# Turned x tiles in PSUM tiles of their own, and the x loads in another place of the queue

## The chip, the cores and the metric

The kernel runs on one core of one Trainium2 chip. The metric is the device time of one execution in microseconds (us), the median of several. A profile is one execution, recorded by the hardware; its "span" is about 1.7 us shorter than the device time of the same execution.

TensorE is called PE in the profile, its weight loads PEld, VectorE DVE, ScalarE ACT, GpSimd POOL, SyncE SP (SPq is its queue, from which most DMAs are issued). The profile also gives the clock granted to TensorE as a share of full speed; "cold" below means half speed.

## The reference, cut to what matters

Two independent computations share the output. A is a diagonal state-space layer, B an attention over segments of 32 tokens with a memory of 8 tokens. Both read an x of 2048 tokens by 1024 features.

```
# A: u = x B^T; h[t] = Lam * h[t-1] + u[t]; y = 2 Re(h C^T) + x * Dskip
# B: per segment: h = concat(mem, x_seg); q, k, v = h Wq, h Wk, h Wv (32 heads of 128)
#    o = softmax(q k^T / sqrt(128) + mask) v;  out = o Wo;  mem = out[:8]
```

Only the first 80 us matter here. There the kernel computes the V projection of B in "V quarters" (512 tokens by 4 heads; `v_x`), each in four PSUM tiles of 128 tokens by 512 columns ("V tiles" 0 to 3), and, interleaved with them, the u of A (`stage1`), whose scan runs on VectorE and whose states go to DRAM (`a_hs`).

## The kernel before

TensorE needs the features of x on the partitions, so x must be turned. For the first 512 tokens of B the kernel loads x plainly (`b_xr`) and turns it on TensorE into PSUM, from where VectorE and ScalarE copy it to `b_xe`. All later quarters of x, for B (`b_xe`) and A (`a_xT`), are turned by DMA transposes issued from SyncE.

```python
# class K: tag "U" has 2 buffers of 4 KiB per partition, "P" has 3 of 2 KiB
def turn_x0(self, i):                      # i = 0..3: 128 tokens each
    k = self.k
    if i % 2 == 0:
        self.xt = k.ps("U", (128, 2, KC, 128), BF16)      # one tile for two turns
    for c in range(KC):
        k.PE.transpose(self.xt[:, i % 2, c, :], self.x0[i][:, c * 128:(c + 1) * 128], k.ident[:])
    for h in range(2):                                     # halves: "v" VectorE, "s" ScalarE
        cs = slice(4 * h, 4 * h + 4)
        k.copy("vs"[h], self.xe[:, cs, 128 * i:128 * i + 128], self.xt[:, i % 2, cs, :])

# v_x, first quarter only:
    ps = [k.ps("P")[:] for _ in range(3)]
    self.turn_x0(0); self.turn_x0(1)
    for i, c in ((0, 0), (0, 1), (1, 0), (1, 1)):
        self.v_mm(ps[i], w, i, 128 * c, 128 * c + 128)     # V tiles 0 and 1, columns 0 to 255
    self.turn_x0(2)
    self.v_mm(ps[0], w, 0, 256, 512); self.v_mm(ps[1], w, 1, 256, 512)
    self.turn_x0(3)
    ps.append(k.ps("U", (128, 2, 512))[:, 0, :])
    self.v_mm(ps[2], w, 2); self.v_mm(ps[3], w, 3)         # V tiles 2 and 3

# check_consts, called late in the program, but hoisted by the scheduler to the start:
    k.fmask = k.cst.tile([L, 2, L], FP32, name="f_mask")
    G.memset(k.fmask[:], 1.0)                              # ... more on GpSimd (G) ...
    V.tensor_scalar(k.fmask[:, 1, :], k.fmask[:, 0, :], 1.0, 1.0e9, ALU.subtract, ALU.mult)   # on VectorE

# the main loop; steps alternate: v v v v, then s v s v ...   ("s" is stage1 of A)
    b.load_x(1)
    # ... consts, parameters ...
    b.v_x(0, 0, wv[0])
    a.load_b(0); a.load_x(0)
    loads = [lambda: b.load_x(2), lambda: a.load_x(1), lambda: a.load_x(2), lambda: b.load_x(3), lambda: a.load_x(3)]
    for kind, pc, q in order[1:]:
        if loads and kind == "v":
            loads.pop(0)()
        # ... v_x, or stage1, which ends with: SP.dma_start(self.hs[tb][:, pc, :, :], h[:])
```

PE and SP are pinned to program order in this phase; the other engines are ordered by the scheduler.

## Time and profile before

| | before |
|---|---|
| device time, median of 3 | 1260.05 us (1259.23 to 1260.36) |
| PE busy | 1239.0 of 1257.7 us |
| PE idle, for copies of turned x | 6.2 us, twice, longest 5.1 |
| PE idle, for the DMA of A's last x quarter | 1.6 us, once |

From the page, the summary of PE:

```profile
PE 1239.0 (99%) x8270; PEld 664.0 (53%) x8342; DVE 668.2 (53%) x1248; ACT 263.7 (21%) x633; POOL 273.4 (22%) x407
```

PE's waits in the kernel before (engine, line, what it would do next, what ended the wait; us in total, times, longest):

```profile
PE psU L62 <- ACT b_xe L87: 6.2, 2, 5.1
PE psU L62 <- DMA a_xT<-in_A_x_dram: 1.6, 1, 1.6
```

The timeline of PE (start us, duration us, what, and in brackets the idle time before it):

```profile
9.03 0.61 PE L62 MATMUL psU<-ident,b_xr 128*128 128x128 bf16 x8
16.47 1.01 PE L62 MATMUL psU<-ident,b_xr 128*128 128x128 bf16 x8 [5.09 <-ACT b_xe L87]
17.70 3.19 PE L62 MATMUL psP<-b_wv,b_xe 128*128 128x512 bf16 x7 [0.22 <-issue]
23.13 0.18 PE L62 MATMUL psR<-ident,a_r 24*128 24x24 bf16 x1
...
77.41 3.63 PE L62 MATMUL psU<-a_xT,a_bt 128*128 128x512 bf16 x16 [1.58 <-DMA a_xT<-in_A_x_dram]
```

After 11.4 us PE idles 5.09 us until a ScalarE copy. The next lines are slow: 8 transposes take 1.01 us that took 0.61 at 9.03; the granted clock is at half from 15.1 to 21.9 us. (At 17.70 one of 8 matmul records is missing, hence "x7"; V tile 2 began near 17.3.) At 77.41 it waits for a_xT.

VectorE, then ScalarE, at the end of that long wait (the same view for each):

```profile
15.29 0.18 DVE L937 TENSOR_SCALAR f_mask<-f_mask 40x40 f32<-40x40 f32 x1 [7.62 <-POOL f_mask L936]
15.38 0.41 DVE L89 COPY b_xe<-psU 128x512 bf16<-128x512 bf16 x1
```

```profile
15.82 0.60 ACT L87 ACTIVATE b_xe<-psU 128x512 bf16<-128x512 bf16 x1 [7.53 <-DVE b_xe L89]
```

Two things are to be seen. ScalarE's half of a copy starts only when VectorE's half has ended (15.38 + 0.41 = 15.79, then 15.82; in the first turn 5.83, then 5.87). The Trainium skill, "PSUM — Partial Sum Buffer" (PSUM bank collisions raise a hardware error), says that two engines must not touch one PSUM bank in the same 32-partition quadrant at once, and that one guards by bank and quadrant (in the simple version by bank), not by address; a turned tile of 8 x 128 bf16 on 128 partitions is one bank of 2 KiB. The trace is in line with such a guard: the halves are never abreast. And the copy at 15.38 is late because VectorE, which works in order, stood 7.62 us in front of `f_mask`, waiting for GpSimd. The skill's "TensorE: Matmul & The Clock Gate" (the engine queue depths in Part 1) calls VectorE's queue strict FIFO; here the copy's data were there from about 9.7 us, and it ran 0.09 us after `f_mask`.

SyncE's queue before:

```profile
26.68 11.05 SPq L62 DMA_TRANSPOSE a_xT<-in_A_x_dram  x2
56.47 0.34 SPq L62 DMA_DIRECT2D a_hs<-a_h  x1
56.85 6.50 SPq L62 DMA_TRANSPOSE b_xe<-in_B_x_dram  x3
67.01 0.33 SPq L62 DMA_DIRECT2D a_hs<-a_h  x1
67.39 6.41 SPq L62 DMA_TRANSPOSE a_xT<-in_A_x_dram  x1
```

The transposes of the first line were issued by 37.7 us. From there to 56.5 the queue stands behind the first store of states, which waits 18.7 us for VectorE's `a_h`; the last transposes come after it.

### The profile page before, as it was taken

What the parts mean: (1) busy time and instruction counts of PE and PEld (TensorE: products, weight loads), DVE (VectorE), ACT (ScalarE), POOL (GpSimd) and SP (SyncE); (2) the same over time, 40 slices, a digit from 0 to 9 for tenths busy, and PEclk for the clock granted to TensorE, in tenths of its full rate; (3) what the DMA queues carried; (4) which work ended last, traced back from release to release, by engine and by line L of the source; (5) the groups of instructions that cost most, each with busy time, mean ns of one, the idle gap of its engine ahead of it and who ended that gap; (6) DMA issues with size and microseconds to landing.
All of it is one profiled execution on the core that took longest, in us unless ns stands there. A gap on an engine that the chain in (4) does not pass through costs nothing.

```text
span 1257.7 us, 20118 instructions
## 1 busy us (share of the span) xinstructions
PE 1239.0 (99%) x8270; PEld 664.0 (53%) x8342; DVE 668.2 (53%) x1248; ACT 263.7 (21%) x633; POOL 273.4 (22%) x407
## 2 busy tenths in 40 slices
PE   7999999999999999999999999999999999999998
PEld 4444444444455555566666666556665654446444
DVE  3578999898811123666666666666666641001000
ACT  3543444443320000121211121111211110000000
POOL 3012321212332220322222222222323220000000
PEclk8999999999999999999999999999999999999999
DMA  9695524574698939245464454545474279407000
GB/s 244 163 227 144 163 88 124 158 163 132 166 327 254 276 103 264 78 91 140 105 146 105 114 132 103 130 96 121 95 160 90 58 221 218 112 17 152 17 17 27
DMA packets 314744, 174.18 MB, mean 138 GB/s; under 512 B 138648, under 2 KB 300048, under 8 KB 314648
## 3 DMA queue, kind: packets, MB, share of 16 engines
q1 hardware_dynamic: 292552, 146.22, 48.2%
q10 hardware_dynamic: 21072, 23.47, 5.7%
q0 software_dynamic: 1024, 3.17, 0.7%
q8 instruction: 66, 1.08, 0.4%
q14 instruction: 30, 0.25, 0.1%
HBM read 87.47 MB, written 52.19 MB: 111 GB/s over the span
## 4 chain that ended last, share of the span: by engine, by line
PE 96%; POOL 1%; DMA 1%; DVE 1%; issue 1%; ACT 0%; SPq 0%; POOLq 0%; ACTq 0%; DVEq 0%
PE psP L62 80%; PE psU L62 9%; PE psS L62 3%; PE psO L62 2%; PE psR L62 2%; DMA a_xT<-in_A_x_dram 1%; POOL b_m L642 0%; DVE a_pr L273 0%; DVE a_pr L265 0%; POOL a_r L163 0%; ACT b_e L639 0%; DVE a_n L284 0%; DVE a_pr L268 0%; POOL maskB L123 0%; POOL maskA L123 0%
## 5 line engine op out<-in xcount | busy, mean ns | idle before, releaser
L62 PE MATMUL psP<-b_xe,b_wq 128*128 128x480 bf16 (+1 forms) x1280 | 247.8, 343 | 0.1
L62 PE MATMUL psP<-b_xe,b_wk 128*128 128x480 bf16 (+1 forms) x1280 | 247.7, 343 | 0.0
L62 PE MATMUL psP<-b_wv,b_xe 128*128 128x512 bf16 (+2 forms) x1033 | 224.9, 374 | 1.0 <-issue 0.2
L642 POOL TENSOR_TENSOR b_m<-b_e,maskB 99x396 bf16<-99x396 bf16 x160 | 139.4, 871 | 336.5 <-ACT b_e L639 336.5
L639 ACT ACTIVATE b_e<-psS 99x396 bf16<-99x396 f32 x176 | 88.0, 500 | 534.5 <-PE psS L62 528.6
L62 PEld LDWEIGHTS <-b_wk 128*128 128x128 bf16 x1280 | 119.2, 98 | 94.6
L62 PEld LDWEIGHTS <-b_xe 128*128 128x128 bf16 x1056 | 102.4, 98 | 120.8 <-issue 3.2
L62 PEld LDWEIGHTS <-b_wq 128*128 128x128 bf16 x1280 | 118.5, 97 | 88.2
L89 DVE CAST b_k<-psP 128x480 bf16<-128x480 f32 (+1 forms) x192 | 98.1, 532 | 100.2 <-PE psP L62 100.2
L89 DVE CAST b_q<-psP 128x480 bf16<-128x480 f32 (+1 forms) x192 | 98.1, 533 | 93.7 <-PE psP L62 92.0
L62 PEld LDWEIGHTS <-b_ol 128*128 128x128 bf16 x864 | 84.2, 98 | 94.5
L62 PE MATMUL psU<-a_xT,a_bt 128*128 128x512 bf16 x493 | 113.9, 379 | 2.6 <-DMA a_xT<-in_A_x_dram 1.6
L62 PE MATMUL psP<-t,a_hl 128*128 128x512 bf16 x496 | 112.1, 379 | 0.8
L89 DVE CAST b_ost<-psP 128x512 bf16<-128x512 f32 (+1 forms) x17 | 11.5, 676 | 183.4 <-PE psP L62 182.4
L62 PE MATMUL psP<-wo,b_ol 128*128 128x512 bf16 (+1 forms) x440 | 91.9, 364 | 0.4
L62 PE MATMUL psP<-t,b_ol 128*128 128x512 bf16 x408 | 91.7, 379 | 0.4
L278 POOL TENSOR_SCALAR a_tt<-a_pr,a_tabf 128x1 f32<-128x1 f32 x48 | 34.0, 709 | 253.6 <-DVE a_pr L273 253.6
L87 ACT ACTIVATE b_vst<-psP 128x512 bf16<-128x512 f32 x126 | 72.2, 591 | 74.6 <-PE psP L62 67.6
L659 DVE TENSOR_TENSOR b_ob<-psO,b_accR 99x384 bf16<-99x384 f32 x160 | 85.9, 553 | 2.2
L265 DVE TENSOR_TENSOR a_pr<-psU,a_tabf 128x2048 f32<-128x2048 f32 x32 | 73.1, 2283 | 17.9 <-PE psU L62 16.2
L62 PEld LDWEIGHTS <-a_bt 128*128 128x128 bf16 x512 | 49.1, 98 | 59.3 <-DMA a_xT<-in_A_x_dram 1.7
L62 PEld LDWEIGHTS <-a_hl 128*128 128x128 bf16 x512 | 49.0, 98 | 56.7
(198 smaller groups left out, 965.6 us busy)
## 6 DMA issues: line engine op xcount, KB each, us to landing
b_v<-b_vx SPq DMA_DIRECT2D x16, 1064.2 KB
b_wv<-in_B_Wv_dram SPq DMA_DIRECT2D x16, 1024.0 KB
b_on<-b_ob SPq DMA_DIRECT2D x15, 960.0 KB
b_vx<-b_vst ACTq DMA_DIRECT2D x24, 516.0 KB
a_hs<-a_h SPq DMA_DIRECT2D x32, 256.0 KB
b_wog<-in_B_Wo_dram SPq DMA_DIRECT2D x4, 2048.0 KB
b_wq<-in_B_Wq_dram SPq DMA_DIRECT2D x16, 512.0 KB
b_wk<-in_B_Wk_dram SPq DMA_DIRECT2D x16, 512.0 KB
```

The costliest lines, as they stand in the source:

```text
L62: r = f(*a, **kw)
L87: self.S.activation(out, in_, ACT.Copy)
L89: self.V.tensor_copy(out, in_)
L265: V.tensor_tensor(pr[:], u[:].unsqueeze(1).to_broadcast([128, 2, 2, TB]), view(t3, [[TB + 1, 2], [TB + 1, 2], [1, TB]]), ALU.mult)
L278: G.tensor_scalar(tt[:, j:j + 1], w[:, j, TB - 1:TB], t3[:, 1, TB:TB + 1], None, ALU.mult)
L639: k.S.activation(e[:], s[0:GW], ACT.Exp, scale=float(E) ** -0.5, accum_out=self.accE[0:GW, i:i + 1])
L642: k.G.tensor_tensor(m[:, 0:4 * GW].rearrange("p (a b q) -> p a b q", a=2, b=2), e[:], mask[0:GW, :, :].unsqueeze(2).to_broadcast([GW, 2, 2 ...
L659: V.tensor_tensor(self.ob[:, b0:b0 + n, :], o[0:GW, 0:n, 0:E], r.unsqueeze(2).to_broadcast([GW, n, E]), ALU.mult)
```

## The change

Three parts: each turn gets a PSUM tile of its own and one engine copies it whole; the second x quarter of B is loaded behind the first V quarter; all x loads stand in front of the first store of states.

```diff
     def turn_x0(self, i):
         k = self.k
-        if i % 2 == 0:
-            self.xt = k.ps("U", (128, 2, KC, 128), BF16)
+        pt = k.ps("U", (128, 2, KC, 128), BF16)[:, 0, :, :]
         for c in range(KC):
-            k.PE.transpose(self.xt[:, i % 2, c, :], self.x0[i][:, c * 128:(c + 1) * 128], k.ident[:])
-        for h in range(2):
-            cs = slice(4 * h, 4 * h + 4)
-            k.copy("vs"[h], self.xe[:, cs, 128 * i:128 * i + 128], self.xt[:, i % 2, cs, :])
+            k.PE.transpose(pt[:, c, :], self.x0[i][:, c * 128:(c + 1) * 128], k.ident[:])
+        k.copy("vs"[i % 2], self.xe[:, :, 128 * i:128 * i + 128], pt)
 ...
-            b.load_x(1)
             consts(k)
 ...
             b.v_x(0, 0, wv[0])
+            b.load_x(1)
 ...
-            loads = [lambda: b.load_x(2), lambda: a.load_x(1), lambda: a.load_x(2), lambda: b.load_x(3), lambda: a.load_x(3)]
+            loads = [[(b, 2)], [(a, 1), (a, 2)], [(b, 3), (a, 3)]]
 ...
                 if loads and kind == "v":
-                    loads.pop(0)()
+                    for o, n in loads.pop(0):
+                        o.load_x(n)
```

## The prediction

> **Bound.** TensorE: the page gives it 1239 of 1257.7 us (99%), the chain of waits 96%. Only PE idle and cold-clock time can be won. PE's waits are few: 6.2 us (2 times, longest 5.1) for the ScalarE copies of turned x into b_xe, 1.6 us once for the DMA transpose of A's last x quarter (a_xT), 1.3 us at the start, 0.8 us later.
>
> **1. Turned x (timeline, first 25 us).** Before, the halves of one PSUM tile are copied in series: VectorE 0.42 us, then ScalarE 0.60 us, then the next transposes, which wait for ScalarE. The big wait has another root: VectorE is in order, and ahead of the third turn's copy stands f_mask, which waits 7.6 us for GpSimd's mask work and runs at 15.29. So that copy starts at 15.38, ScalarE's half ends at 16.42, PE idles 5.1 us to 16.47, does the last transposes (1.01 us, cold), then V tiles 2 and 3, to about 23.1. The changed kernel's instruction order keeps f_mask ahead of that copy: the stall stays. What goes: the last turn, now in the other buffer and copied by ScalarE, runs before the stall; the third copy is one VectorE copy, estimated 0.69 us (0.42 plus 0.27 streaming). PE restarts near 16.15 directly on V tile 2, instead of about 17.3.
>
> The clock takes part of that. The granted clock falls to 0.5 at about 15.2 and returns at about 21.95; the Trainium skill, "TensorE: Matmul & The Clock Gate" (Part 1), says that one idle window of about 3.4 us throttles, one busy one releases, on free-running windows. The trace agrees: 6.8 us is two windows. Idle is now about 11.9 to 16.15, so I expect half speed again, released near 22. Cold 128x512 matmuls take 0.427 us each (tile 2: 3.4 us for 8), warm ones 0.223: 16 from 16.15 end near 22.4, not 23.1. Gain 0.7 us; 2.3 if the clock returns one window earlier, 3.4 if it doesn't fall.
>
> **2. Second x quarter behind the first V quarter.** SyncE's order and waits there are unchanged. Gain 0.
>
> **3. x loads ahead of the first store of states.** Before, SyncE sits 18.7 us behind the store that waits for VectorE's a_h (37.7 to 56.5), while DMA falls idle (0 to 0.5 busy, 40 to 55). Then come the rest of B's x and, behind a second store, a_xT, issued 67.4, landed 77.4: PE idles 1.58 us. Now these transposes issue from about 38 to 51: gain 1.6 us. b_vx stores should fit beside them: V groups are 10 us apart there.
>
> **Does it last?** Afterwards PE is gapless, and VectorE releases the U tiles well before PE needs them (209.3 for a use at 215.8), so an earlier PE stays earlier.
>
> **Prediction.** 0.7 + 1.6 = 2.3 us, with some chance of a kinder clock: 1257.5 us, 80% range 1255.0 to 1259.2. Faster by over 2%: 0.005; within 2%: 0.99; slower: 0.005.
>
> **What would show it.** Right: PE's waits no longer list a_xT; f_mask still runs at 15.3; one PE idle of about 4 us remains, now for VectorE, ending near 16.15; half clock from 15 to 22; V quarter 0 done at 22.4; store of states 0 still at about 56.5, behind the transposes. Wrong: f_mask no longer stalls; the clock stays 1.0; ScalarE's b_vst waiting for DMA; or a new PE wait after 80 us.
>
> **What would make it wrong.** The phase of the clock windows (up to 2.7 us more gain); transposes landing late enough at 40 to 60 us to hold b_vx stores and PSUM evictions; a later DMA wait that eats the lead.

## The result

| | before | after |
|---|---|---|
| device time, median of 4 | 1259.76 us (1259.23 to 1260.36) | 1256.16 us (1255.69 to 1256.97) |
| span of the profiled run | 1257.7 us | 1254.8 us |
| first V quarter's matmuls over (PE goes to the next small matmul) | 23.13 | 21.93 |
| fourth stage of A starts on PE | 77.41 | 74.49 |

The ratio is 0.9972, interval [0.9955, 0.9989]. A ratio is the mean time of one kernel's fast runs over that of the other's of the same rounds, so it is not quite the ratio of the medians quoted. It means 0.1 to 0.5% less: well inside the 2% that count as the same, but clear of zero.

The views after, in the order of those before. The page's PE line, and PE's waits:

```profile
PE 1239.3 (99%) x8270; PEld 664.9 (53%) x8342; DVE 667.6 (53%) x1246; ACT 263.7 (21%) x631; POOL 273.3 (22%) x407
```

```profile
PE psP L62 <- DVE b_xe L89: 4.9, 1, 4.9
```

PE's timeline:

```profile
10.86 0.61 PE L62 MATMUL psU<-ident,b_xr 128*128 128x128 bf16 x8
16.32 3.19 PE L62 MATMUL psP<-b_wv,b_xe 128*128 128x512 bf16 x7 [4.86 <-DVE b_xe L89]
19.31 2.69 PE L62 MATMUL psU<-b_wv,b_xe 128*128 128x512 bf16 x8
21.93 0.18 PE L62 MATMUL psR<-ident,a_r 24*128 24x24 bf16 x1
...
74.49 3.61 PE L62 MATMUL psU<-a_xT,a_bt 128*128 128x512 bf16 x16
```

The last turn now runs at 10.86, before the stall; the stall is still there, listed as 4.86 us; and a_xT is no longer waited for. One matmul record is missing at 16.32 ("x7"): V tile 3 starts at 19.31, and eight matmuls at 0.427 us before that is 15.9, which is when VectorE's copy ends, so the stall is nearer 4.4 us:

```profile
15.09 0.18 DVE L934 TENSOR_SCALAR f_mask<-f_mask 40x40 f32<-40x40 f32 x1 [8.30 <-POOL f_mask L933]
15.19 0.68 DVE L89 COPY b_xe<-psU 128x1024 bf16<-128x1024 bf16 x1
```

SyncE:

```profile
39.52 9.09 SPq L62 DMA_TRANSPOSE b_xe<-in_B_x_dram  x3
48.65 4.56 SPq L62 DMA_TRANSPOSE a_xT<-in_A_x_dram  x1
55.27 0.34 SPq L62 DMA_DIRECT2D a_hs<-a_h  x1
```

The transposes that stood behind the two stores are issued by 53.2 us, and the store of states at 55.27 is not held by them.

The two steps at the bottom of the table are the whole of the gain: 1.20 us at the first V quarter (23.13 to 21.93), 1.72 us more at the fourth stage of A (2.92 in all), and nothing afterwards (the spans differ by 2.9).

### The profile page after: what moved, and what is told of

It reads as the page before. It is cut to its first block, busy times and chain, and to the rows that moved or that the text cites. A ratio compares the mean times of both kernels' runs of the same rounds, so it can differ in the third digit from the quotient of the medians.

```text
span 1254.8 us, 20111 instructions
## 1 busy us (share of the span) xinstructions
PE 1239.3 (99%) x8270; PEld 664.9 (53%) x8342; DVE 667.6 (53%) x1246; ACT 263.7 (21%) x631; POOL 273.3 (22%) x407
## 3 DMA queue, kind: packets, MB, share of 16 engines
q0 software_dynamic: 1024, 3.17, 0.7%
## 4 chain that ended last, share of the span: by engine, by line
PE 98%; POOL 1%; issue 1%; ACT 0%; DVE 0%; POOLq 0%; ACTq 0%
PE psP L62 81%; PE psU L62 9%; PE psS L62 3%; PE psO L62 2%; PE psR L62 2%; POOL b_m L639 0%; POOL a_r L163 0%; ACT b_e L636 0%; POOL maskB L123 0%; POOL maskA L123 0%; POOL maskB L122 0%; DVE b_xe L89 0%; POOL c_skip L927 0%; POOL maskB L129 0%; POOL maskA L122 0%
```

## The experiments

All outputs are right.

### e1: the turned tiles alone

On the kernel before, the first hunk of the change and nothing else:

```diff
-        if i % 2 == 0:
-            self.xt = k.ps("U", (128, 2, KC, 128), BF16)
+        pt = k.ps("U", (128, 2, KC, 128), BF16)[:, 0, :, :]
 ...  (turn into pt)
+        k.copy("vs"[i % 2], self.xe[:, :, 128 * i:128 * i + 128], pt)     # for the two half copies
```

> The kernel before with the turned x tiles alone (own PSUM tiles, copied whole). Theory: it restarts PE near 15.9 us directly on V tile 2 and ends the first V quarter about 1.2 us earlier (21.9 instead of 23.1); the a_xT wait near 77 us stays. But then PE is 1.2 us earlier against a load whose time is set by VectorE's store of states (which itself moves earlier with PE), so the gain is 1.0 to 1.3 us. Rival (the whole gain comes from the loads): 0. Rival (the third part wins less and the turns more): over 2 us.

Measured: 1259.14 us against 1259.91; ratio 0.999, interval [0.9976, 1.0004], so not clear of zero. PE's timeline, then the load in SyncE's:

```profile
22.21 0.18 PE L62 MATMUL psR<-ident,a_r 24*128 24x24 bf16 x1
77.32 3.63 PE L62 MATMUL psU<-a_xT,a_bt 128*128 128x512 bf16 x16 [2.41 <-DMA a_xT<-in_A_x_dram]
```

```profile
66.48 7.28 SPq L62 DMA_TRANSPOSE a_xT<-in_A_x_dram  x1
```

The first V quarter ended 0.92 us earlier than before (22.21), and the load was issued 0.91 us earlier (66.48 instead of 67.39). But the fourth stage started at 77.32 instead of 77.41: the wait for a_xT had grown from 1.58 to 2.41 us, because the transpose took 10.8 us from its issue to PE's start instead of 10.0. In this trace nothing of the gain was left, and its span is that of before, 1257.7. But that time of the load varies by itself: in e3, whose instructions are those of before, it was 10.5 us. So one trace doesn't tell whether the load always eats the gain (e6 speaks against it), and the times leave room for a gain from 0 to 3 us. How much the tiles are worth without the loads isn't settled.

### e2: the loads' order alone

On the kernel before:

```diff
-            loads = [lambda: b.load_x(2), lambda: a.load_x(1), lambda: a.load_x(2), lambda: b.load_x(3), lambda: a.load_x(3)]
+            loads = [[(b, 2)], [(a, 1), (a, 2)], [(b, 3), (a, 3)]]
 ...  (and the loop over each group, as in the change)
```

> The kernel before with only the order of the x loads changed (the rest of B's x and A's last quarter in front of the first store of states). Theory: the start is as before (PE idle 5.1 us to about 16.5, first V quarter done at 23.1), the 1.58 us wait for a_xT goes, gain 1.6 to 1.8 us; together with the turns the gains add up to the 2.9 us seen between the two spans. Rival (the a_xT wait only moves elsewhere, and all of the gain is in the turns): 0 to 0.5 us.

Measured: 1256.78 us against 1259.91; ratio 0.9973, interval [0.9961, 0.9986]. PE's timeline:

```profile
22.98 0.18 PE L62 MATMUL psR<-ident,a_r 24*128 24x24 bf16 x1
75.54 3.61 PE L62 MATMUL psU<-a_xT,a_bt 128*128 128x512 bf16 x16
```

The profile shows no wait for a_xT; the fourth stage starts at 75.54, 1.87 us earlier than before, and the start is nearly as before (idle 5.15 us, first V quarter over at 22.98, 0.15 us earlier). From the end of the first V quarter to the fourth stage it is 52.56 us here and in the changed kernel, 54.28 before: 1.72 us are the loads' own. So most of the gain is this part. Whether the two parts alone add up, as expected, the times don't settle: by the spans they are 0 (e1) and 1.8 us against 2.9 for both, by the medians 0.8 and 3.1 against 3.6. The difference in time is larger than what the trace shows (1.8 us of span): six runs were 1256.69 to 1257.7, eleven of the kernel before 1258.35 to 1263.69. In part this is because the profiled run is the slowest of the six: it had a mean granted clock of 0.996, while the four fastest (1256.69 to 1256.79) had 0.998 or 0.999, which leaves no room for the 6.8 us at half clock of the profiled start (0.0027 of the span; see e5).

### e3: the second quarter alone

On the kernel before:

```diff
-            b.load_x(1)
             consts(k)
 ...
             b.v_x(0, 0, wv[0])
+            b.load_x(1)
```

> The kernel before with only the second x quarter's load moved behind the first V quarter in the program. Its instructions and semaphore waits are the same on all five engines as before, in the same order, so the theory says 0, and what it shows is the noise of such a comparison: within 0.6 us. A rival that holds that the position of this load matters: over 0.6 us faster.

Measured: 1259.64 us against 1259.91; ratio 0.9997, interval [0.9984, 1.001]. Zero, as the equal instruction streams demand; SyncE is pinned, and between the two places in the program no other DMA is issued from it. It also shows how far two traces of one stream differ: the first V quarter ended at 22.76 (before: 23.13), the wait for a_xT was 2.08 us (1.58), and the span 1257.9 (1257.7).

### e4: f_mask's scaling on GpSimd

On the changed kernel:

```diff
-    V.tensor_scalar(k.fmask[:, 1, :], k.fmask[:, 0, :], 1.0, 1.0e9, ALU.subtract, ALU.mult)
+    G.tensor_scalar(k.fmask[:, 1, :], k.fmask[:, 0, :], 1.0, 1.0e9, ALU.subtract, ALU.mult)
```

> The changed kernel with the one f_mask scaling moved from VectorE to GpSimd, so that VectorE no longer waits for GpSimd ahead of the third turn's copy. Theory (this stall, not the copies, makes the remaining 4.9 us of PE idle and the cold clock that follows): no idle over 1 us after 5 us, clock never halves, first V quarter done at about 15 us instead of 21.9, 5 to 7 us faster than the changed kernel, unless the x loads land too late for it, which would show as PE waits for DMA b_xe or a_xT between 20 and 80 us. Rival (PE waits there for the DMA of x tile 3 or of the V weights, f_mask only being named): under 1 us faster.

Measured: 1249.49 us (1249.28 to 1249.68) against 1259.91 of the kernel before; ratio 0.9914, interval [0.99, 0.9928]. That is 6.7 us less than the 1256.16 that the changed kernel took in another call; the spans differ by 7.0 (1254.8 and 1247.8), and so do the ends of the first V quarter. PE's timeline:

```profile
11.38 1.89 PE L62 MATMUL psP<-b_wv,b_xe 128*128 128x512 bf16 x8
13.11 1.89 PE L62 MATMUL psU<-b_wv,b_xe 128*128 128x512 bf16 x8
14.93 0.18 PE L62 MATMUL psR<-ident,a_r 24*128 24x24 bf16 x1
```

The last turn runs at 10.93, V tile 2 follows it without a gap, at the full clock (1.89 us for 8 matmuls with the drain of the last), and the quarter is over at 14.93 instead of 21.93. The x loads landed in time for it. The rival falls: neither x tile 3 nor the weights were late. This is the best version that was run.

### e5: the changed kernel again

> The changed kernel once more, unaltered, as the yardstick for the other runs of this call and for the two parts alone. Expected: 1256 us, 3.0 to 3.6 us faster than the kernel before, PE idle of 4.9 us once, no wait for a_xT.

Measured: 1255.84 us against 1259.71; ratio 0.997. The same kernel, but its first V quarter was over at 21.19, not 21.93:

```profile
21.19 0.18 PE L62 MATMUL psR<-ident,a_r 24*128 24x24 bf16 x1
```

The views by stretches of time show why (span of the stretch, its length, busy us of PE, PEld, DVE, ACT, POOL with counts, then the granted clock, the DMA share and GB/s). First the changed kernel's first profile, then this one:

```profile
14.00:15.00 1.00, 0.00 (x0) 0.00 (x0) 0.00 (x0) 0.00 (x0) 0.86 (x7) 0.55 1.31 300
19.00:20.00 1.00, 1.00 (x4) 0.34 (x3) 0.00 (x0) 0.45 (x1) 0.00 (x0) 0.50 0.78 162
```

```profile
14.00:15.00 1.00, 0.00 (x0) 0.00 (x0) 0.00 (x0) 0.00 (x0) 0.86 (x7) 1.00 1.27 290
19.00:20.00 1.00, 1.00 (x5) 0.39 (x4) 0.00 (x0) 0.43 (x1) 0.00 (x0) 0.80 1.12 195
```

In finer stretches of 0.2 us the clock is at half from 14.1 to 20.9 us in the first, and from 16.0 to 19.4 in the second: 6.8 and 3.4 us. The Trainium skill ("TensorE: Matmul & The Clock Gate", Part 1) describes free-running windows of about 3.4 us, of which an idle one throttles and a busy one releases; these numbers are two windows and one. The fall came at 15.1, 14.1, 14.4, 14.9 and 14.3 us in before, after, e1, e2 and e3, each for two windows, and at 16.0, 16.5 and 15.9 in e5, e9 and e10, each for one. So the stall is about as long in all of them (4.4 to 5.5 us), but its bill depends on where the window stands.

### e6: the mask alone, on the kernel before

```diff
-    V.tensor_scalar(k.fmask[:, 1, :], ...)      # kernel before
+    G.tensor_scalar(k.fmask[:, 1, :], ...)
```

> The kernel before (neither turns nor loads changed) with f_mask's scaling moved to GpSimd. Theory (the load of a_xT is an anchor: what the start gains, PE mostly waits away near 77 us while the load stands behind two stores): the first V quarter ends at about 15.5 us instead of 23.1, but PE's wait for a_xT grows from 1.6 us to 4 us or more, so of 7.5 us gained at the start at most 5 remain: 1255 or slower. Rival (the load moves along with the stores, which move with PE): the wait stays at 1.5 to 2 us and 7 us remain, about 1252.5.

Measured: 1254.61 us (1251.89 to 1255.36) against 1259.71; ratio 0.9955, interval [0.9941, 0.9969]. PE's timeline, then two stretches of time with the columns of e5:

```profile
15.56 0.18 PE L62 MATMUL psR<-ident,a_r 24*128 24x24 bf16 x1
70.57 5.31 PE L62 MATMUL psU<-a_xT,a_bt 128*128 128x512 bf16 x16 [2.31 <-DMA a_xT<-in_A_x_dram]
```

```profile
71.00:72.00 1.00, 1.00 (x4) 0.39 (x3) 0.00 (x0) 0.00 (x0) 0.00 (x0) 0.50 1.10 362
75.00:76.00 1.00, 1.00 (x7) 0.45 (x5) 0.08 (x1) 0.00 (x0) 0.00 (x0) 1.00 1.17 257
```

Both theories miss. The wait is 2.31 us, not 4: the load follows the second store, which follows PE, and it was issued 7.57 us earlier (59.82) and landed 6.8 us earlier, so the rival has the mechanism. But the time is the theory's, because of something that neither foresaw: around this wait the clock fell, from 71.0 to 74.4 us, and the 16 matmuls that follow took 5.31 instead of 3.63 us. Of 7.57 us gained at the start 0.7 went to a longer wait and 1.7 to the clock; 5.1 are left in the span. In e1 the wait was longer (2.41 us) and the clock stayed at 1.00, so the length of the wait alone doesn't decide. The quickest run of the five (1251.89) had a mean granted clock of 1.000, the others 0.997 or 0.998. A wait for a late load in this place thus costs 1.6 to 2.4 us, and sometimes 1.7 more. Whether the tail of the kernel before (up to 1263.69, with a mean clock of 0.996) comes from this too is not shown: no profile caught it, and e2's profiled run had 0.996 without such a fall, since a fall in the last us of the run counts in the mean too.

### e7: the mask and the loads, with the old tiles

```diff
-    V.tensor_scalar(k.fmask[:, 1, :], ...)      # kernel of e2
+    G.tensor_scalar(k.fmask[:, 1, :], ...)
```

> The kernel before with the x loads moved and f_mask's scaling on GpSimd, but the turned tiles as before (shared in pairs, copied in halves). Theory (the turned tiles matter mainly because they take the last turn from behind the f_mask stall): without the stall they are worth only the serial copies of the first pair, so this is within 0.8 us of the changed kernel with f_mask on GpSimd, 1249.5 to 1250.5. Rival (the tiles are worth their 1.2 us on their own): 1250.7 or slower.

Measured: 1250.16 us (1249.66 to 1251.62) against 1259.71; ratio 0.9924, interval [0.991, 0.9937]. Against e4, of another call, that is 0.7 us by the medians and 1.3 by the ratios, so the theory's 0.8 is neither confirmed nor refuted. The runs form two groups: three at 1249.66 to 1250.16, two at 1251.6. The profile caught one of the latter. PE's timeline of e7, then the same place in e6, which has the same tiles:

```profile
6.87 1.01 PE L62 MATMUL psU<-ident,b_xr 128*128 128x128 bf16 x8 [1.14 <-ACT b_xe L87]
7.67 3.36 PE L62 MATMUL psP<-b_wv,b_xe 128*128 128x128 bf16 x32
```

```profile
6.86 0.61 PE L62 MATMUL psU<-ident,b_xr 128*128 128x128 bf16 x8 [1.14 <-ACT b_xe L87]
7.31 2.23 PE L62 MATMUL psP<-b_wv,b_xe 128*128 128x128 bf16 x32
```

In both PE waits 1.14 us for ScalarE's half before the second turn, but in e7 the work after it ran slowly (32 matmuls of 128 columns in 3.36 us, in e6 2.23), as it does at half clock. The granted clock reads 1.00 there, so that the clock hadn't been released yet is argued from the speed alone. If so, this is one more use of separate tiles: they remove that 1.14 us gap in the very stretch in which the clock warms up.

### e8: PE kept busy during the stall

On the changed kernel:

```diff
             self.turn_x0(3)
+            pw = k.ps("R")
+            for _ in range(16):
+                k.PE.matmul(pw[:], self.x0[3][:, 0:128], self.x0[3][:, 0:512], start=True, stop=True)
```

> The changed kernel with 16 idle-filling matmuls of 512 columns (into a PSUM tile that nothing reads) behind the last turn, so that PE is busy from 11.5 to about 15.0 us of the f_mask stall, which itself stays. Theory (the half clock after the stall costs 12 cold matmuls at 0.427 instead of 0.223 us): the clock stays at 1.0, V tiles 2 and 3 take 3.6 us instead of 6.0 and end at about 19.5 instead of 21.9, and the kernel is 2.2 to 2.6 us faster than the changed one, 1253.7. Rival (V tiles 2 and 3 are slow for another reason, for example their weights still landing): no gain, under 0.5 us.

Measured: 1255.17 us, against 1255.84 of the changed kernel (e5). At the stage the theory holds: the clock stayed at 1.00 through the stall and V tiles 2 and 3 took 3.56 us (16.09 to 19.65), against 6.0 in the first profile of the changed kernel and 5.3 in e5. But of the 1.54 us gained over e5 only 0.64 was left at A's first stage (41.62 against 42.26). The end of the quarter on PE, then ScalarE's timeline and PE's waits, show where some of it went:

```profile
19.65 0.18 PE L62 MATMUL psR<-ident,a_r 24*128 24x24 bf16 x1
```

```profile
32.15 1.58 ACT L87 ACTIVATE b_vst<-psP 128x512 bf16<-128x512 f32 x3 [1.33 <-DMA b_xe<-in_B_x_dram]
```

```profile
PE psP L62 <- ACT b_vst L87: 0.5, 1, 0.5
```

The compiled programs show that the edit changed which semaphores the DMAs share: ScalarE's store of V ahead of these copies shares one with an x transpose of `b_xe` here, and with a transpose of `a_bt` in the changed kernel. By the profile ScalarE now waits 1.33 us for the x transpose, in the stream with its store of V, and PE in turn 0.54 us for one of the copies out of PSUM; neither wait is in e5. That is 0.54 of the 0.90 us lost; the other 0.36 are in no listed wait of PE. So the cold clock costs what was said at the stage, but its removal in this way paid only 0.7 us. The miss is in the total, and more than half of it is a side effect of the edit.

### e9: tiles of their own, copied in halves

```diff
-        k.copy("vs"[i % 2], self.xe[:, :, 128 * i:128 * i + 128], pt)
+        for h in range(2):
+            cs = slice(4 * h, 4 * h + 4)
+            k.copy("vs"[h], self.xe[:, cs, 128 * i:128 * i + 128], pt[:, cs, :])
```

> The changed kernel, but each turned tile copied in halves by VectorE and ScalarE, one after the other, as before; the tiles stay separate. Theory (the separate tile is what takes the last turn from behind the f_mask stall; whole copies only take ScalarE's 0.6 us out of the restart): the last turn still runs before 12 us, PE restarts directly on V tile 2 but near 16.3 us instead of 15.9; 0.4 us slower than the changed kernel, which the phase of the clock can hide in the total. Rival (the whole copies do the work): the last turn runs after the stall, as before, and the total is like loads alone, 1256.8 or more.

### e10: tiles shared in pairs, copied whole

```diff
-        pt = k.ps("U", (128, 2, KC, 128), BF16)[:, 0, :, :]
+        if i % 2 == 0:
+            self.xt = k.ps("U", (128, 2, KC, 128), BF16)
 ...  (transposes into self.xt[:, i % 2], one copy of that half by one engine)
```

> The changed kernel, but turned tiles shared in pairs as before, each half of the pair copied whole by one engine. Theory: the last turn waits for VectorE's copy of the third and runs after the stall, cold, from about 15.9 us (0.85 us for its 8 transposes), so V tile 2 starts near 16.8 instead of 15.9, half a us better than the kernel before (17.3). Rival (whole copies do the work): the last turn runs before 12 us and V tile 2 starts near 15.9.

Measured: 1256.24 us (e9) and 1256.04 (e10) against 1260.08, ratios 0.9968 and 0.9965: by time neither can be told from the changed kernel. Their timelines can; e9 first, then e10:

```profile
10.64 0.61 PE L62 MATMUL psU<-ident,b_xr 128*128 128x128 bf16 x8
15.68 2.78 PE L62 MATMUL psP<-b_wv,b_xe 128*128 128x512 bf16 x8 [4.43 <-DVE b_xe L89]
```

```profile
15.92 1.01 PE L62 MATMUL psU<-ident,b_xr 128*128 128x128 bf16 x8 [4.43 <-DVE b_xe L89]
16.73 3.19 PE L62 MATMUL psP<-b_wv,b_xe 128*128 128x512 bf16 x8
```

The separate tile takes the last turn out of the stall (10.64 in e9); the whole copy does not (15.92 in e10, and V tile 2 starts at 16.73, as expected). The expectation for e9 was wrong in one point: PE restarted at 15.68, earlier than with whole copies (15.9), not later. The first four of the eight matmuls of V tile 2 need VectorE's half only, which ended at 15.62, so halves let PE start sooner. With separate tiles the whole copies therefore gain nothing. With shared tiles they do: V tile 2 starts at 16.73 in e10, and at 17.22 and 17.32 in e2 and e3, which share the tiles and copy halves. Of the 1.4 us from about 17.3 to 15.9, whole copies alone give about 0.5 and the separate tile the rest, or all of it when the copies stay halves.

## Why the prediction was right

The forecast of 1257.5 us, range 1255.0 to 1259.2, holds the measured 1256.16.

- PE's two waits were the right place to look, and f_mask's stall stayed, as said: PE idles 4.4 us (listed as 4.9), now for VectorE. Its removal (e4) was worth 6.7 us more.
- The restart was forecast near 16.15 and came near 15.9. The copy took 0.68 us (estimate 0.69); f_mask ran at 15.09 instead of 15.29.
- The first term, 0.7 us, was 1.20 in the profiled run and would be 1.94 in e5. The cold clock was foreseen, and its 6.8 us too, but its release "near 22" carried the window's position from one trace to another: it came at 20.9, and at 19.4 in e5. That the term came out at 1.20 and not at 1.94 was the luck of that phase. The Trainium skill says that the window is free-running, and the prediction cited it without drawing this consequence for its main case.
- The second term, 0, was right (e3).
- The third term, 1.6 us, was 1.72 in the trace and also alone (e2, without the 0.15 us of its start). The transposes were issued by 53.2 instead of 51 us, and neither the b_vx stores nor PSUM evictions made PE wait.
- "An earlier PE stays earlier" held from 75 us to the end: 2.92 us there, 2.9 in the spans.
- What the sum left out: the terms stand in series, and the wait for a_xT isn't a constant. It was 1.58, 2.08, 2.31 and 2.41 us in four traces, took all of the start's 0.92 us in e1, and tripped the clock for 1.7 us more in e6. The prediction costed the idle time of one trace, not its spread. That spread may be why the measured gain, 3.6 us by the medians, is above the 2.3 forecast and above the 2.9 of the two profiled runs; how the spread splits between this wait and the clock at the start was not measured. For the changed kernel, which has no such wait, the mean clocks point to the start: its five runs at 0.998, in which two windows at half clock don't fit, took 1255.49 to 1255.86 us, its four at 0.997 1256.42 to 1256.97.

## What to carry to other kernels

When PE waits for a copy, look at what that engine did just before: here a tiny constant, hoisted by the scheduler onto an in-order engine, held the copy back for over 5 us, and moving that one instruction to the engine that it waited for gained 6.7 us (5.1 on the kernel before), where the rearrangement of tiles gained about one at its stage. A gain in front of a late load is sure only once the load no longer binds, so move both. A PE wait of a few us costs its idle time and sometimes a half-speed clock of 3.4 or 6.8 us, depending on a phase that the kernel doesn't control; judge such changes by the stage's timeline in several profiles, not by one.

## What the Trainium skill lacked or had wrong

- "TensorE: Matmul & The Clock Gate" (Part 1) speaks of an idle window that throttles. In e6 the clock fell after a window of 3.4 us (67.6 to 71.0) in which PE is recorded as busy for 1.09 us, much of it with 4-column matmuls. How little activity counts as idle is not stated.
- The same page puts the return of the clock at around 4 us into sustained activity, give or take 0.5 us between runs. Here it came 5.5 us (before), 5.0 us (after) and 3.5 us (e5) after PE's restart. These figures fit windows that don't release when they begin with idle time: the one from 15.1 to 18.5 us in before was idle up to 16.47 and didn't, the one from 16.0 to 19.4 in e5 was busy and did. The range to reckon with is wider than the 0.5 us of that sentence.
- The page warns that clock records are unreliable. Here they fit the matmuls' speed, except at the start: the clock reads 1.00 from 0 us, while the first 8 matmuls of 512 columns take 3.60 us in before, 0.45 each.
- "DMA: Bandwidth & Descriptors" (DMA Transpose (X-bar)) doesn't say how long a large transpose holds the queue that issues it. One of 512 x 1024 bf16 held SyncE's queue for 4.2 to 8.6 us in these traces, and the one of a_xT that PE waited for took 10.0 to 10.8 us from issue to PE's use of it. Everything behind it in the queue waits.
